# Chunked attention and a normalised feed-forward layer on one core: the z of the last tile turned by VectorE and sixteen transfers instead of by TensorE

## The chip, the cores and the metric

The kernel runs on one core of a Trainium2 chip. The metric is the device time of one execution in microseconds (us). Three runs of the kernel before took 499.17, 499.29 and 499.5 us; the median is 499.29 us. The engines are TensorE (PE in the profile; its weight loads are PEld), VectorE (DVE), ScalarE (ACT), GpSimd (POOL) and SyncE (SP). SP, ACT and POOL each have an instruction queue from which DMA transfers are issued; in the profile these issues are rows of SPq, ACTq and POOLq, or rows of POOL named DMA_DIRECT2D.

## The reference

Attention runs inside chunks of 64 positions, for 8 batches, 8 heads, 576 positions and a head size of 64. Its output, laid out as 4608 tokens of 512 numbers, goes through a feed-forward layer with a SoLU and a layer norm:

```python
scores = scale * q_c @ k_c^T                  # per chunk of 64
attn = softmax(scores);  x = attn @ v_c       # x: 4608 x 512
h = x @ w_in                                  # 4608 x 1024
solu = h * softmax(h)                         # along the row
ln = (solu - mean) / sqrt(var + 1e-06) * g_ln
out = ln @ w_out                              # 4608 x 512
```

All inputs and outputs are float32.

## The kernel before, in words

The 4608 tokens are 36 tiles of 128 tokens, numbered 0 to 35 (`NT` is 36, `P` is 128). Each tile goes through the same stages: scores, softmax and values of its two chunks, then `ffn_in` (the product with `w_in` into the PSUM tile `ph`), `solu_a` and `solu_b` (softmax times h, centred, into the SBUF tile `z`), `variance` (two ScalarE squares and two small GpSimd operations, which give the row factor `r`), the turning of `z` so that its 1024 columns lie on the partitions, `ffn_out` (the product with `w_out` into the PSUM tile `po`), and `store` (ScalarE scales `po` by `r` into `o_sb`, and a transfer writes it out).

Each float32 factor of the two big products is split into a high and a low part, and a product is three passes: high by low, high by high, low by high. So `ffn_out` needs the turned z as two tiles, `ZH` (`z_h` in the profile) and `ZL` (`z_l`). There is one of each for the whole kernel. They are filled in two halves in the last tiles: columns chunks 0 to 3 and 4 to 7 of the eight chunks `fc`. A half of `ZH` can be overwritten only when the products of the tile before have read it.

`ffn_out` of one tile is 24 products of 128x512, three to a chunk `fc`, in the order of `fc`. It is cut into three parts of 8 products each. The list `queue` holds the parts that are not yet issued, and runs three tiles behind `ffn_in`: while tile i is in `ffn_in`, the three parts of tile i-3 are issued between its steps. After the loop over tiles is through, the last `while queue` loop issues what is left, the parts of tiles 33, 34 and 35. In iteration 35 and in this last loop the parts go through `third_ahead`, which after part 1 fills the first half of `ZH` and `ZL` for the next tile (`z_half(m + 1, 0)`), and after part 2 the second half, and then stores the tile. The last tile's `ffn_out` is cut by columns as well: 48 products of 128x256, half of them into a `po` tile and half into a bank of the PSUM tile `TP` (`tp` in the profile), which the function `bank` hands out in turn, two banks in all.

There are two ways from `z` to `ZH` and `ZL`, and `direct(m)` in line 703 says which a tile takes:

- For all tiles but 0, 1 and 35: `z_turn` (line 586). One VectorE transpose turns each 32x32 block in place and writes slot `i % 2` of the SBUF tile `z_b`. Sixteen transfers, eight on SP's queue and eight on POOL's, then carry the blocks to their partitions in the tile `z_t`. `z_b` and `z_t` have two slots each, interleaved in memory, for an even tile and the odd one after it; a pair of tiles is carried at once, after the odd one. Tile 34, whose partner is direct, is carried alone, with half the bytes. `z_split` (line 611) then makes `ZH` with a ScalarE copy and `ZL` with a VectorE subtraction, both reading one slot of `z_t`.
- For tiles 0, 1 and 35: `z_transpose` (line 619). TensorE turns four 128x128 blocks into a bank of `TP`, ScalarE copies the bank into a half of `ZH`, VectorE subtracts for the half of `ZL`; twice, once for each half.

The instructions of each engine stand in the order in which the program writes them: the class `Order` fixes that for TensorE, VectorE, ScalarE, GpSimd and SyncE. Only the transfers that `store_rest` issues through `nc.scalar` have their place chosen by the planner. All these operations are recorded at line 49, the helper, so the rows of the profile are told apart by tile names. Waits between engines are put in by the tile framework from what each instruction reads and writes.

In iteration 35, the order around the change is: `ffn_in(35)`, `solu_a(35)`, part 0 of tile 32, `solu_b(35)`, part 1 of tile 32 with the first half for tile 33, `variance(35)`, part 2 of tile 32 with the second half for tile 33 and the scaling of tile 32, and `store_rest`. Then come tiles 33, 34 and 35 in the last loop.

Of the kernel before, what the change touches and what calls it, by code (L numbers as in the profile page):

```python
# [8 lines left out]
F32 = mybir.dt.float32  # L9
# [48 lines left out]
def chunk_attention_then_solu_ffn(  # L58
# [14 lines left out]
    P = 128  # L73
# [4 lines left out]
    NT = B * S // P  # L78
    NCC = DM // P
    NFC = FF // P  # L80
# [14 lines left out]
    work = ctx.enter_context(tc.tile_pool(name="work", bufs=2))  # L95
# [251 lines left out]
    def load_v(i):  # L347
        V[i] = work.tile([P, H, D], F32, name="v_sb", bufs=4)
        for p0, p1, b, s in tile_parts(i):
            sync.dma_start(  # L350
                V[i][p0:p1], v[b, :, s:s + p1 - p0, :].rearrange("h t d -> t h d")
            )
# [19 lines left out]
    st = {}  # L372
# [43 lines left out]
    def softmax_e(i):  # L416
        e = st[i, "e"]
        act.activation(e, e, AF.Exp, scale=SCALE)

    def softmax_b(i):  # L420
        e = st[i, "e"]
        ssum = small.tile([P, H], F32, name="s_sum")
        if order.on or i in (6, 7):
            dve.tensor_reduce(out=ssum, in_=ES[i % 2], axis=AX.X, op=ALU.add)
        else:
            dve.tensor_reduce(out=ssum, in_=e, axis=AX.X, op=ALU.add)
            dve.tensor_scalar(
                out=ssum, in0=ssum, scalar1=1e-9, scalar2=None, op0=ALU.add
            )
        rinv = small.tile([P, H], F32, name="s_rinv")  # L430
        dve.reciprocal(out=rinv, in_=ssum)
        dve.tensor_tensor(
            out=e, in0=e, in1=rinv.unsqueeze(2).to_broadcast([P, H, CH]), op=ALU.mult,
        )
# [25 lines left out]
    def attn_turn(i):  # L460
        a = st.pop((i, "e"))
        if i % 2 == 0:
            turned["a"] = work.tile([P, 2, 2, H, 32], F32, name="a_b", bufs=1)
        ab = turned["a"]
        dve.transpose(
            out=ab[:, :, i % 2].rearrange("p y h t -> p h y t"),
            in_=a.rearrange("p h (y k) -> p h y k", k=32),
        )
        if i % 2 == 1:
            for c in range(2):  # L470
                for x in range(2):
                    for y in range(2):
                        to, of = c * CH + x * 32, c * CH + y * 32
                        (pool if x == y else sync).dma_start(
                            AT[to:to + 32, y].rearrange("p s h t -> p (s h t)"),
                            ab[of:of + 32, x].rearrange("p s h t -> p (s h t)"),
                        )
# [27 lines left out]
    def x_high(i):  # L505
        xv = attn(i)[:, :, 1].rearrange("p c a t -> p a c t")
        xh = work.tile([P, NCC, P], F32R, name="x_h")
        xl = work.tile([P, NCC, P], F32R, name="x_l")
        xhv, xlv = (x.rearrange("p a (c t) -> p a c t", t=CH) for x in (xh, xl))
        act.copy(xhv, xv)  # L510
        st[i, "x"] = xh, xl
# [6 lines left out]
    def ffn_in(i):  # L518
        xh, xl = st[i, "x"]
        ph = st[i, "h"] = ps_h.tile([P, 2, HALF], F32, name="ph")  # L520

        sums = [(n, cc, m) for n in range(2) for cc in range(NCC) for m in range(3)]
        if i == 0:
            sums.sort(key=lambda s: s[1])
        else:

            sums.sort(key=lambda s: (s[0], s[2] == 2))
        for at, (n, cc, m) in enumerate(sums):
            if i == 0 and at and at % 6 == 0:
                yield  # L530
            cols = slice(n * HALF, (n + 1) * HALF)
            x, w = ((xh, wi_l), (xh, wi_h), (xl, wi_h))[m]
            pe.matmul(
                ph[:, n, :], x[:, cc, :], w[:, cc, cols],
                start=(cc == 0 and m == 0), stop=(cc == NCC - 1 and m == 2),
            )
# [31 lines left out]
    def variance(i):  # L568
        z, esum = st.pop((i, "z"))

        eps = small.tile([P, 1], F32, name="eps")
        act.activation(eps, esum, AF.Square, scale=1e-3, bias=tiny)
        sq = work.tile([P, FF], mybir.dt.bfloat16, name="sq", bufs=1)
        ssq = small.tile([P, 1], F32, name="ssq")
        act.activation(sq, z, AF.Square, scale=1.0 / (FF * 32), accum_out=ssq)
        u = small.tile([P, 1], F32, name="u")
        pool.tensor_tensor(out=u, in0=ssq, in1=eps, op=ALU.add)
        r = small.tile([P, 1], F32, name="r", bufs=7)
        pool.tensor_tensor(out=r, in0=u, in1=mhalf, op=ALU.pow)
        st[i, "n"] = (z, r)  # L580
# [3 lines left out]
    turned = {}  # L584

    def z_turn(i):
        z, _ = st[i, "n"]
        if i % 2 == 0:
            turned["b"] = work.tile([P, 4, 2, NFC, 32], F32, name="z_b", bufs=1)
        zb = turned["b"]  # L590
        dve.transpose(
            out=zb[:, :, i % 2, :, :].rearrange("p q a t -> p a q t"),
            in_=z.rearrange("p (a q c) -> p a q c", q=4, c=32),
        )
        alone = direct(i + 1)
        if i % 2 == 1 or alone:
            zt = work.tile([P, 4, 2, NFC, 32], F32, name="z_t")
            of = slice(0, 1 if alone else 2)
            for x in range(4):
                for y in range(4):  # L600
                    (pool if (x + y) % 2 else sync).dma_start(
                        zt[x * 32:(x + 1) * 32, y, of].rearrange("p s a t -> p (s a t)"),
                        zb[y * 32:(y + 1) * 32, x, of].rearrange("p s a t -> p (s a t)"),
                    )
            for m in (i,) if alone else (i - 1, i):
                st[m, "zr"] = zt
# [4 lines left out]
    def z_split(i, f):  # L611
        zt = st[i, "zr"][:, :, i % 2, :, :].rearrange("p y a t -> p a y t")
        zhv, zlv = (x.rearrange("p a (y t) -> p a y t", t=32) for x in (ZH, ZL))
        act.copy(zhv[:, f], zt[:, f])
        dve.tensor_tensor(
            out=zlv[:, f], in0=zt[:, f], in1=zhv[:, f].bitcast(F32), op=ALU.subtract
        )
# [76 lines left out]
    def load_some(n):  # L694
        for f, *args in loads[:n]:
            f(*args)
        del loads[:n]

    def load_batch(b):
        loads.extend(qk_loads(b))  # L700


    def direct(m):
        return m < 2 or m == NT - 1

    queue = [(m, p) for m in range(NT) for p in range(3)]

# [7 lines left out]
    def third():  # L715
        m, p = queue.pop(0)
        ffn_out(m, p, 3)
        if p == 2:
            store(m)
# [12 lines left out]
    def whole(parts):  # L732
        for _ in parts:
            pass
# [39 lines left out]
    for i in range(first, NT):  # L774
        order.on = i >= ORD
        odd = i % 2 == 1
        if i == first:
            z_turn(i - 1)
            load_batch(next_batch)
            next_batch += 1  # L780
        if i + 3 < NT:
            load_v(i + 3)
        z_split(queue[0][0], slice(0, NFC))
        if not odd:

            if i + 3 < NT:
                softmax_e(i + 3)
                softmax_b(i + 3)
                attn_turn(i + 3)
            if i + 1 < NT:  # L790
                x_high(i + 1)
        load_some(LOADS[0])
        whole(ffn_in(i))

        if odd:
            for m in (i + 1, i + 2):
                if m + 2 < NT:
                    scores(m + 2)
                if m < NT:
                    values(m)  # L800
        whole(solu_a(i))

        def part():
            if i == NT - 1:
                third_ahead()
            else:
                third()

        part()
        if odd:  # L810
            if i + 3 < NT:
                softmax_a(i + 3)
                softmax_e(i + 3)
            if i + 1 < NT:
                x_high(i + 1)
        elif i + 1 < NT:
            x_low(i + 1)
        whole(solu_b(i))
        if odd:
            if i + 1 < NT:  # L820
                x_low(i + 1)
            if i + 3 < NT:
                softmax_b(i + 3)
                attn_turn(i + 3)
        else:
            for m in (i + 4, i + 5):
                if m < NT:
                    turn(m)
        part()
        variance(i)  # L830
        part()
        load_some(LOADS[1])
        if not direct(i):
            z_turn(i)
        store_rest()
        if odd and i + 4 < NT:
            softmax_a(i + 4)
# [34 lines left out]
```

## Time and profile before

| | |
|---|---|
| Median of the runs | 499.29 us (499.17 to 499.5) |
| Profiled execution: its span, first to last instruction | 496.9 us |
| Median of the runs less that span | 2.39 us |
| TensorE busy | 474.8 us, 96% of the span |
| VectorE busy | 382.4 us, 77% |
| ScalarE busy | 263.1 us, 53% |
| GpSimd busy | 144.6 us, 29% |
| Mean granted TensorE clock | 0.998 |

The record of the profiled execution holds its span, and no device time of its own beside it. Times in rows of the timeline and of the chain are microseconds from the span's start. A row of the timeline gives the start, the duration, the engine, the line, the operation with the tile written and the tiles read, the shapes, and how many instructions are merged; in brackets stands the idle time of the engine before it and what ended that. Matmuls are pipelined: a row of 0.39 us follows another after 0.23 us, so the distance between two starts is what a product costs.

### The profile page before, as it was taken

The page shows a single profiled execution, that of the slowest core. Times are in us where ns is not written, and L with a number is a line of the kernel's source. Part 1 is how long each engine was busy: PE and PEld are TensorE (multiplying, and loading weights), DVE is VectorE, ACT ScalarE, POOL GpSimd, SP SyncE. Part 2 cuts the span into 40 slices and gives each one's busy share as a digit, 9 for nine tenths or more (in the row PEclk, how much of TensorE's full clock was granted, in tenths as well). Part 3 has the DMA queues.
Part 4 walks back from the last instruction along what each step waited for, and adds up shares of the span by engine and source line. Part 5 has one row for each costly group of instructions (what it writes and reads, how often), then busy time and mean ns, then how long its engine had stood idle before and what let it go on. Part 6 is the DMA issues. An engine that isn't in the chain of part 4 may idle for free.

```text
span 496.9 us, 11143 instructions
## 1 busy us (share of the span) xinstructions
PE 474.8 (96%) x4232; PEld 387.5 (78%) x4232; DVE 382.4 (77%) x535; ACT 263.1 (53%) x436; POOL 144.6 (29%) x298
## 2 busy tenths in 40 slices
PE   2899699999999999999999999999999999999995
PEld 1577577888888888888888888888888888888875
DVE  2899897778786988787888788887979797944420
ACT  3687784554644455454554545454545454545441
POOL 0134321515050515051414232332323232413300
PEclk9999999999999999999999999999999999999999
DMA  9999894466868678687718596868662525343211
GB/s 263 285 298 246 143 148 89 108 131 165 152 171 150 167 138 199 126 194 126 181 39 196 107 204 128 211 100 197 135 166 63 151 76 139 85 108 106 65 42 42
DMA packets 195908, 72.57 MB, mean 146 GB/s; under 512 B 180048, under 2 KB 180560, under 8 KB 195472
## 3 DMA queue, kind: packets, MB, share of 16 engines
q1 hardware_dynamic: 189008, 58.49, 54.1%
q0 software_dynamic: 6272, 12.60, 9.7%
q8 instruction: 33, 0.54, 0.5%
q10 hardware_dynamic: 576, 0.79, 0.4%
q14 instruction: 19, 0.16, 0.1%
HBM read 37.23 MB, written 9.44 MB: 94 GB/s over the span
## 4 chain that ended last, share of the span: by engine, by line
PE 89%; DVE 4%; ACT 2%; DMA 2%; issue 1%; SPq 1%; POOL 0%; ACTq 0%; DVEq 0%; POOLq 0%
PE po L49 40%; PE ph L49 38%; PE tp L49 6%; PE sx L49 4%; DMA nat<-in_q_dram 2%; SPq L49 1%; DVE w_r L49 1%; DVE w_p L49 1%; ACT z_h L49 1%; ACT attn_t L49 1%; DVE z_l L49 1%; DVE wi_l L49 0%; DVE h_nmax L49 0%; DVE w_a L49 0%; DVE z L49 0%
## 5 line engine op out<-in xcount | busy, mean ns | idle before, releaser
L49 PE MATMUL po<-wo_l,z_h 128*128 128x512 f32 (+1 forms) x288 | 113.4, 394 | 0.1
L49 PE MATMUL ph<-wi_l,x_h 128*128 128x512 f32 x288 | 112.6, 391 | 0.7 <-DVE z L49 0.6
L49 PE MATMUL ph<-wi_h,x_h 128*128 128x512 f32 x288 | 112.1, 389 | 0.0
L49 PE MATMUL po<-wo_h,z_l 128*128 128x512 f32 (+1 forms) x288 | 111.7, 388 | 0.0
L49 PE MATMUL po<-wo_h,z_h 128*128 128x512 f32 (+1 forms) x288 | 111.6, 388 | 0.0
L49 ACT ACTIVATE z<-ph,h_nmax 128x1024 f32<-128x1024 f32 x36 | 40.2, 1117 | 133.2 <-DVE h_nmax L49 132.7
L49 PE MATMUL ph<-wi_h,x_l 128*128 128x512 f32 x288 | 78.0, 389 | 0.0
L49 POOL TENSOR_TENSOR u<-ssq,eps 128x1 f32<-128x1 f32 x36 | 7.2, 199 | 232.8 <-ACT sq L49 232.7
L49 POOL DMA_DIRECT2D z_t<-z_b x136 | 67.9, 506 | 17.6 <-DVE z_b L49 14.8
L49 DVE TENSOR_REDUCE h_nmax<-ph 128x1 f32<-128x1024 f32 x36 | 44.0, 1223 | 33.8 <-PE ph L49 33.8
L49 PEld LDWEIGHTS ph<-wi_l,x_h 128*128 128x128 f32 x288 | 54.1, 188 | 12.2 <-PE sx L49 0.7
L49 PEld LDWEIGHTS po<-wo_l,z_h 128*128 128x128 f32 x288 | 54.1, 188 | 11.8 <-ACT z_h L49 0.5
L49 PEld LDWEIGHTS po<-wo_h,z_l 128*128 128x128 f32 x288 | 54.1, 188 | 11.6 <-DVE z_l L49 0.4
L49 PEld LDWEIGHTS ph<-wi_h,x_l 128*128 128x128 f32 x288 | 54.1, 188 | 11.3
L49 PEld LDWEIGHTS ph<-wi_h,x_h 128*128 128x128 f32 x288 | 54.1, 188 | 11.1
L49 PEld LDWEIGHTS po<-wo_h,z_h 128*128 128x128 f32 x288 | 54.1, 188 | 10.4
L49 DVE TENSOR_TENSOR z_l<-z_t,z_h 128x1024 fp32r<-128x1024 f32 (+1 forms) x35 | 40.7, 1163 | 20.9 <-ACT z_h L49 20.9
L49 DVE SCALAR_TENSOR_TENSOR z<-ph,z 128x1024 f32<-128x1024 f32 x36 | 43.9, 1221 | 14.1 <-ACT z L49 14.1
L49 ACT ACTIVATE z<-z,z_sum 128x1024 f32<-128x1024 f32 x32 | 36.9, 1154 | 22.1 <-DVE z L49 21.6
L49 DVE STREAM_TRANSPOSE z_b<-z 128x1024 f32<-128x1024 f32 x33 | 40.0, 1211 | 3.3 <-ACT z L49 3.1
L49 ACT ACTIVATE o_sb<-po,r 128x512 f32<-128x512 f32 (+1 forms) x36 | 24.3, 675 | 29.2 <-POOL r L49 20.3
L49 ACT ACTIVATE sq<-z 128x1024 bf16<-128x1024 f32 x36 | 37.6, 1043 | 2.2 <-POOL z L49 2.2
(101 smaller groups left out, 638.9 us busy)
## 6 DMA issues: line engine op xcount, KB each, us to landing
out_dram<-o_sb SPq DMA_DIRECT2D x33, 256.0 KB, 2.5
v_sb<-in_v_dram SPq DMA_DIRECT2D x32, 256.0 KB, 4.3
z_t<-z_b SPq DMA_DIRECT2D x128, 64.0 KB, 2.9
z_t<-z_b POOLq DMA_DIRECT2D x128, 64.0 KB, 2.6
q_st<-in_q_dram SPq DMA_DIRECT2D x96, 72.0 KB, 3.2
k_st<-in_k_dram SPq DMA_DIRECT2D x96, 72.0 KB, 3.2
w_raw<-in_moe_w_out_dram SPq DMA_DIRECT2D x4, 1024.0 KB, 6.6
attn_t<-a_b SPq DMA_DIRECT2D x60, 64.0 KB, 3.7
```

Source lines behind the costliest of these rows:

```text
L49: ins = make(*args, **kwargs)
```

## The change

Tile 35 no longer takes the direct way. It shares the `z_t` tile of tile 34, in the other slot, but is carried by sixteen transfers of its own, as tile 34 is by its sixteen. Its `z_turn` is called in iteration 35 after part 1 of tile 32 and ahead of `variance(35)`, so it reads `z` where `solu_b` left it. Tiles 0 and 1 stay direct.

```diff
     def z_turn(i):
-        z, _ = st[i, "n"]
+        z, _ = st.get((i, "n")) or st[i, "z"]
...
-        alone = direct(i + 1)
+        alone = i >= NT - 2
         if i % 2 == 1 or alone:
-            zt = work.tile([P, 4, 2, NFC, 32], F32, name="z_t")
-            of = slice(0, 1 if alone else 2)
+            if i < NT - 1:
+                turned["t"] = work.tile([P, 4, 2, NFC, 32], F32, name="z_t")
+            zt = turned["t"]
+            of = slice(i % 2, i % 2 + 1) if alone else slice(0, 2)
             for x in range(4):
                 for y in range(4):
                     (pool if (x + y) % 2 else sync).dma_start(
...
     def direct(m):
-        return m < 2 or m == NT - 1
+        return m < 2
...
         part()
+        if i == NT - 1:
+            z_turn(i)
         variance(i)
         part()
         load_some(LOADS[1])
-        if not direct(i):
+        if i < NT - 1:
             z_turn(i)
```

## The prediction

> **What bounds the kernel now.** I read the page first, then the chain of waits, then the timeline of the tail engine by engine. The page says which engine sets the end:
>
> ```profile
> span 496.9 us, 11143 instructions
> PE 89%; DVE 4%; ACT 2%; DMA 2%; issue 1%; SPq 1%; POOL 0%; ACTq 0%; DVEq 0%; POOLq 0%
> ```
>
> TensorE carries 89% of the chain. So an edit counts only by what it takes from or adds to TensorE's row of products, and this one touches only the tail. The chain there, start and duration:
>
> ```profile
> 485.94 0.59 ACT z_h L49
> 486.53 0.03 issue
> 486.56 0.70 DVE z_l L49
> 487.26 0.04 issue
> ```
>
> The reader is to see that the chain leaves TensorE for ScalarE and VectorE and comes back to it 0.04 after 487.26, within tile 35. The timeline of TensorE gives the prices; the two rows "tp<-ident,z x4" are the 8 transposes, between the products:
>
> ```profile
> 479.15 0.39 PE L49 MATMUL po<-wo_h,z_l 128*128 128x512 f32 x1
> 479.38 0.39 PE L49 MATMUL po<-wo_l,z_h 128*128 128x512 f32 x1
> ...
> 481.87 0.39 PE L49 MATMUL po<-wo_h,z_l 128*128 128x512 f32 x1
> ...
> 482.78 0.39 PE L49 MATMUL po<-wo_l,z_h 128*128 128x512 f32 x1
> 483.01 0.60 PE L49 MATMUL tp<-ident,z 128*128 128x128 f32 x4
> 483.36 0.48 PE L49 MATMUL po<-wo_h,z_h 128*128 128x512 f32 x1
> ...
> 485.07 0.39 PE L49 MATMUL po<-wo_h,z_l 128*128 128x512 f32 x1
> 485.30 0.60 PE L49 MATMUL tp<-ident,z 128*128 128x128 f32 x4
> 485.66 0.36 PE L49 MATMUL po<-wo_l,z_h 128*128 128x256 f32 x1
> 487.30 0.38 PE L49 MATMUL tp<-wo_l,z_h 128*128 128x256 f32 x1 [1.28 <-DVE z_l L49]
> 487.52 0.28 PE L49 MATMUL po<-wo_h,z_h 128*128 128x256 f32 x1
> 487.64 0.28 PE L49 MATMUL tp<-wo_h,z_h 128*128 128x256 f32 x1
> ...
> 492.92 0.28 PE L49 MATMUL tp<-wo_h,z_l 128*128 128x256 f32 x1
> ```
>
> Tile 34 is the 24 products from 479.38 to 485.07, tile 35 the 48 half products from 485.66 to 492.92. Two paces follow: 16 products start from 479.38 to 482.78, so (482.78 - 479.38) / 15 = 0.227 us each; the fourth to the last half product start from 487.64 to 492.92, 44 steps, 0.120 us each.
>
> **What the change removes.** (1) Two groups of four transposes: the step from 482.78 to 483.36 is 0.58 and that from 485.07 to 485.66 is 0.59, where 0.227 would do: 0.35 + 0.36 = 0.71 us. (2) The wait ahead of the first half product into `tp`: 487.30 - 485.66 - 0.12 = 1.52 us. It ends with the second `z_l` of tile 35, which reads `tp`; without transposes nothing of tile 35 reads `tp`, and the half product has nobody there to wait for. (3) Slower steps just behind the transposes and the wait: the seven steps from 483.36 to 485.07 take 1.71 where 7 x 0.227 = 1.59, and 487.30 to 487.52 is 0.22 where 0.12 would do: 0.12 + 0.10 = 0.22 us. Together **2.45 us**. The same by the dense row: tile 34's last product starts at 479.38 + 23 x 0.227 = 484.60, tile 35's first at 484.82 and its last at 484.82 + 47 x 0.120 = 490.46, against 492.92. What follows the last product (two scalings, two stores) keeps its length.
>
> **What it adds, and whether that is hidden.** One VectorE transpose, sixteen transfers, and ScalarE and VectorE reading `z_t` where they read `tp`. The nearest rows are tile 34's own turn and the splits of tiles 33 and 34:
>
> ```profile
> 462.12 1.25 DVE L49 STREAM_TRANSPOSE z_b<-z 128x1024 f32<-128x1024 f32 x1 [1.22 <-ACT z L49]
> 463.39 4.94 SPq L49 DMA_DIRECT2D z_t<-z_b  x8
> 464.49 3.98 POOL L49 DMA_DIRECT2D z_t<-z_b  x8 [0.27 <-issue]
> 471.81 1.15 ACT L49 ACTIVATE z<-z,z_sum 128x1024 f32<-128x1024 f32 x1 [1.30 <-DVE z L49]
> 472.87 0.60 ACT L49 CAST z_h<-z_t 128x512 fp32r<-128x512 f32 x1
> 473.51 0.69 DVE L49 TENSOR_TENSOR z_l<-z_t,z_h 128x512 fp32r<-128x512 f32 x1 [1.73 <-ACT z_h L49]
> 473.53 0.50 PE L49 MATMUL po<-wo_l,z_h 128*128 128x512 f32 x1
> 474.59 0.39 PE L49 MATMUL po<-wo_l,z_h 128*128 128x512 f32 x1
> 475.26 0.69 DVE L49 TENSOR_TENSOR z_l<-z_t,z_h 128x512 fp32r<-128x512 f32 x1 [1.06 <-ACT z_h L49]
> 479.35 0.62 ACT L49 CAST z_h<-z_t 128x512 fp32r<-128x512 f32 x1 [2.10 <-PE po L49]
> 480.00 0.69 DVE L49 TENSOR_TENSOR z_l<-z_t,z_h 128x512 fp32r<-128x512 f32 x1 [2.03 <-ACT z_h L49]
> ```
>
> z of tile 35 is complete at 471.81 + 1.15 = 472.96. On VectorE the transpose stands behind the `z_l` of tile 33's first half, which ends at 473.51 + 0.69 = 474.20, so it runs from 474.20 to 475.45. Behind it is `z_l` of tile 33's second half, due at 475.26: 0.19 us late, so it ends at 476.14. Its first reader is tile 33's fifteenth product; the first starts at 473.53, the fourth at 474.59, the fifteenth 11 x 0.227 later, at 477.09. Free.
>
> The transfers: tile 34's first SP issue came 0.02 after its transpose ended. Here SP issues from 475.47, eight in 4.94 us, the last at 475.47 + 7 x 0.62 = 479.8. POOL takes 3.98 for eight. From issue to landing, from the list of DMA issues in the tail and, below it, the summary of all `z_t` instructions of the kernel:
>
> ```profile
> z_t<-z_b SPq DMA_DIRECT2D x8, 32.0 KB, 1.9
> z_t<-z_b POOLq DMA_DIRECT2D x8, 32.0 KB, 1.7
> DMA to landing us min/median/max: 1.7/2.8/4.5
> ```
>
> The likely landing is 479.8 + 1.9 = 481.7; I take it since those rows have the same size and neighbours. The far end is 479.8 + 4.5 = 484.3.
>
> The first `z_h` of tile 35 overwrites a half that tile 34's twelfth product, at 481.87, reads last. At the tile boundary before, `z_h` at 479.35 came 0.20 after the start of the product at 479.15, so TensorE frees the half at 482.07, after the likely landing. From `z_h` to the end of `z_l` are 480.00 - 479.35 + 0.69 = 1.34 us, so both are there at 483.41. TensorE asks for that `z_h` at 484.82 and for that `z_l` four half products later, at 485.30; the landing may slip to 485.30 - 1.34 = **483.96** before TensorE waits at all. By the far landing, 484.3, it waits 0.34 us and the gain is 2.1. The second half: freed at 484.60 + 0.20 = 484.80, `z_h` ready at 485.42, `z_l` at 486.14, asked for at 484.82 + 24 x 0.120 = 487.70. Free.
>
> Two queues are passed, and each instruction on them is late by the issues ahead of it:
>
> ```profile
> 475.06 0.56 POOL L49 TENSOR_TENSOR r<-u,mhalf 128x1 f32<-128x1 f32 x1
> ```
>
> On POOL, `u` and `r` of tile 35 now stand behind eight issues: `r` ends a little after 475.47 + 3.98 + 0.56 = 480.0 instead of at 475.62, and its first user is a scaling behind the last products, after 490. On SP the store of tile 32 moves behind the eight issues too, to 475.47 + 4.94 = 480.4. The two `o_sb` buffers take turns, so the scaling of tile 34, due when its last product is through at 484.80, needs that store landed; it has 4.4 us for that, and no product of tile 34 or 35 waits for that scaling. On ScalarE the `z_h` that waits for the landing has only the second `z_h` and tile 34's scaling behind it, both due no sooner than 484.80. All of it costs nothing while the landing is before 483.96.
>
> The sum: 496.9 - 2.45 = 494.45 us for the span. The median of the runs is 2.39 us above the span shown, which I carry over unchanged: 499.29 - 2.45 = **496.84 us**.
>
> **Rivals.** *A, the slots are not kept apart (slower).* Tile 34's split reads slot 0 of `z_t`, and in program order it now stands behind the transfers into slot 1 of the same tile. The slots are interleaved; if the waits are made for the whole stretch that the read covers, tile 34's first `z_h` must wait for tile 35's transfers.
>
> ```profile
> 476.63 0.62 ACT L49 CAST z_h<-z_t 128x512 fp32r<-128x512 f32 x1 [0.82 <-PE po L49]
> 484.26 0.69 DVE L49 TENSOR_TENSOR z_l<-tp,z_h 128x512 fp32r<-128x512 f32 x1 [3.57 <-ACT z_h L49]
> ```
>
> It would start at 481.7 instead of 476.63. At tile 33 `z_h` led the first product by 473.53 - 472.87 = 0.66 us, so tile 34 would start at 482.36 instead of 479.38, 2.98 late, and its third product waits for `z_l` as tile 33's did: there the first three products took 474.59 - 473.53 = 1.06 us where 0.68 would do. That is 2.98 + 0.38 = 3.36 lost for 2.45 won: 500.2 us, and 502.8 with the far landing. It becomes a loss once the transfers land after 480.8. For it: the half product at 487.30 waited until the second `z_l` was done, though by the code its bank is that of the first, done at 484.26 + 0.69 = 484.95; so waits are wider than the data there. Against it: `z_h` at 476.63 overwrote its half of `ZH` while tile 33 was still reading the other half (until 479.15), so SBUF parts are told apart, if not interleaved ones.
>
> *B, the transfers land late.* If they land 1 us after 483.96 the time is 497.8; all is lost only with a landing at 486.4, 6.6 us after the last issue, against 4.5 for the slowest of the kernel. Against it: tile 34's sixteen transfers, of the same size and issued in the same way, landed in 1.9 and 1.7. The Trainium skill, page "VectorE: DVE Perf Modes", section "Rules for kernel authors", says to turn a 128x128 block on TensorE where a result in PSUM will do, which it does here, and so speaks against this change. The rows bear it out for latency only: from the transposes to `z_h` it took 485.94 - 485.30 = 0.64 us, while the other way takes 481.7 - 474.20 = 7.5; but it has from 472.96 to 483.96.
>
> *C, the wait stays.* If the first half product into `tp` still waited for tile 35's second `z_l` (486.14), 486.18 - 484.94 = 1.24 would be lost again: 498.1 us. Against it: tile 34's first product at 479.38 did not wait for the `z_l` that began at 480.00.
>
> *D, no change.* The end is set by something that the chain does not show, 499.3 us. The chain's unbroken run on TensorE speaks against it.
>
> **How the numbers follow.** Forecast 0.74, A 0.11, B 0.07, C 0.05, D 0.03. Runs of this kernel differ by 0.33 us, and 0.2% (1.0 us) is about what a measurement can tell from no change. The forecast, nearly all of B (0.06) and half of C (0.03) are faster by more: 0.83. C's and B's rest, D and A with the earliest landing (0.04) are within it: 0.10. A with later landings is slower: 0.07. The range goes from 496.4 (the runs' scatter and the paces' rounding below the sum) to 498.2, which takes in the far landing, most of B and C; A and D are left out.
>
> **What would show it.** Right: no `tp<-ident,z` rows in the tail, a VectorE transpose near 474.2, last `z_t` landing before 484, TensorE starting tile 35 near 484.8 with no gap until 490.5. Wrong: tile 34's first `z_h` past 480 with a releaser DMA (A), a gap on TensorE ahead of tile 35 ended by `z_h` (B), or ahead of the first half product into `tp` (C).

## The result, and the profile after

Five runs of the changed kernel have a median of 496.39 us (495.26 to 496.82), five of the kernel before 499.17 us (498.42 to 499.5). The ratio is 0.995, with a 95% interval of 0.9938 to 0.9963: 1.8 to 3.1 us less. The median lies at the lower end of the stated range, 496.4 to 498.2.

The span of the profiled execution fell from 496.9 to 493.5 us, by more than the prediction's 2.45. The tail shows what the change did. The chain of waits after, start and duration:

```profile
471.94 0.61 ACT z_h L49
472.55 0.04 issue
472.59 11.56 PE po L49 x49
484.15 0.12 PE tp L49
484.27 0.12 PE po L49
...
487.87 0.97 PE po L49 x8
```

Before, the chain left TensorE at 485.91 and came back at 487.30. Now it stays on TensorE from tile 33's first product to the scalings behind the last products. TensorE's timeline at tiles 34 and 35:

```profile
478.44 0.39 PE L49 MATMUL po<-wo_l,z_h 128*128 128x512 f32 x1
...
483.65 0.39 PE L49 MATMUL po<-wo_h,z_l 128*128 128x512 f32 x1
483.88 0.28 PE L49 MATMUL po<-wo_l,z_h 128*128 128x256 f32 x1
483.99 0.28 PE L49 MATMUL tp<-wo_l,z_h 128*128 128x256 f32 x1
...
489.51 0.28 PE L49 MATMUL tp<-wo_h,z_l 128*128 128x256 f32 x1
```

Tile 34 takes (483.65 - 478.44) / 23 = 0.227 us a product, tile 35 (489.51 - 483.88) / 47 = 0.120 a half product: both are dense, with nothing between them. From tile 33's first to tile 35's last product it was 492.92 - 473.53 = 19.39 us, and is 489.51 - 472.59 = **16.92**: 2.47 us less. What was added, in the same window, lies beside that:

```profile
473.18 1.24 DVE L49 STREAM_TRANSPOSE z_b<-z 128x1024 f32<-128x1024 f32 x1
474.34 0.67 DVE L49 TENSOR_TENSOR z_l<-z_t,z_h 128x512 fp32r<-128x512 f32 x1
474.44 4.95 SPq L49 DMA_DIRECT2D z_t<-z_b  x8
474.71 3.91 POOL L49 DMA_DIRECT2D z_t<-z_b  x8 [7.20 <-DVE z_b L49]
475.69 0.62 ACT L49 CAST z_h<-z_t 128x512 fp32r<-128x512 f32 x1 [0.82 <-PE po L49]
476.34 0.69 DVE L49 TENSOR_TENSOR z_l<-z_t,z_h 128x512 fp32r<-128x512 f32 x1 [1.33 <-DMA z_t<-z_b]
478.91 0.56 POOL L49 TENSOR_TENSOR r<-u,mhalf 128x1 f32<-128x1 f32 x1
481.13 0.62 ACT L49 CAST z_h<-z_t 128x512 fp32r<-128x512 f32 x1 [1.51 <-PE po L49]
```

The rows at 475.69 and 481.13 are the first `z_h` of tiles 34 and 35. The first began while tile 35's transfers were still being issued; the second waited for TensorE, not for a transfer. The row at 476.34, the first `z_l` of tile 34, names a transfer as what ended its wait. But it began 0.03 us after its `z_h` ended (475.69 + 0.62 = 476.31), as in the kernel before (477.28 against 476.63 + 0.62 = 477.25), and most of tile 35's transfers had not been issued by then: they did not hold it up.

The other 0.94 us of the span lie ahead of tile 33 (473.53 against 472.59), and 0.93 of them ahead of tile 0's first product, where the two programs are alike. The first product into `ph`, before and then after:

```profile
30.14 0.39 PE L49 MATMUL ph<-wi_l,x_h 128*128 128x512 f32 x1
```

```profile
29.21 0.39 PE L49 MATMUL ph<-wi_l,x_h 128*128 128x512 f32 x1
```

Tile 33's first product came between 472.54 and 474.05 in the seven other profiles below whose program is the same up to there; the latest, 474.05, belongs to the run with the other bank, whose clock was lowered for a time early on (last section). Nothing that the change touches lies there, so this part is taken as scatter between executions, and the readings below go by the stretch from tile 33's first to tile 35's last product.

### The profile page after: what moved, and what is told of

It reads as the page before. It is cut to its first block, busy times and chain, and to the rows that moved or that the text cites. A ratio compares the mean times of both kernels' runs of the same rounds, so it can differ in the third digit from the quotient of the medians.

```text
span 493.5 us, 11163 instructions
## 1 busy us (share of the span) xinstructions
PE 473.3 (96%) x4224; PEld 386.3 (78%) x4224; DVE 383.1 (78%) x536; ACT 263.1 (53%) x436; POOL 148.6 (30%) x306
## 4 chain that ended last, share of the span: by engine, by line
PE 89%; DVE 4%; ACT 2%; DMA 2%; issue 1%; SPq 1%; POOL 0%; ACTq 0%; DVEq 0%; POOLq 0%
PE po L49 40%; PE ph L49 39%; PE tp L49 6%; PE sx L49 4%; DMA nat<-in_q_dram 2%; SPq L49 1%; DVE w_r L49 1%; DVE w_p L49 1%; ACT attn_t L49 1%; DVE wi_l L49 0%; ACT z_h L49 0%; DVE h_nmax L49 0%; DVE z_l L49 0%; DVE w_a L49 0%; DVE z L49 0%
## 5 line engine op out<-in xcount | busy, mean ns | idle before, releaser
L49 POOL DMA_DIRECT2D z_t<-z_b x144 | 71.6, 505 | 24.8 <-DVE z_b L49 23.1
L49 DVE TENSOR_TENSOR z_l<-z_t,z_h 128x1024 fp32r<-128x1024 f32 (+1 forms) x37 | 42.1, 1137 | 24.1 <-ACT z_h L49 22.7
L49 DVE STREAM_TRANSPOSE z_b<-z 128x1024 f32<-128x1024 f32 x34 | 41.2, 1211 | 3.3 <-ACT z L49 3.1
L49 ACT CAST z_h<-z_t 128x1024 fp32r<-128x1024 f32 (+1 forms) x37 | 35.8, 969 | 6.5 <-PE po L49 6.5
```

The lines of the kernel that those rows point to most:

```text
L49: ins = make(*args, **kwargs)
```

## The experiments

**The wait alone taken away, transposes kept.** The kernel before with:

```diff
-                ps_o.tile([P, DM], F32, name="po") if x == 0 else bank()
+                ps_o.tile([P, DM], F32, name="po") if x == 0
+                else ps_h.tile([P, 2, HALF], F32, name="ph")[:, 0]
```

> The kernel before, with the transposes kept; only the second column half of tile 35's last product goes into the PSUM tile ph, which is free by then, instead of into a bank of tp. It leaves nothing out. My theory (the gain is the transposes' 0.71 us plus 0.12 us of slower steps, and the wait of the first half product into tp with the slow step behind it, 1.62 us): the wait is gone and nothing else, so from tile 33's first product to tile 35's last it is 19.39 - 1.62 = 17.8 us, and the time is 1.6 us below before. Rival (the product waits for z_l itself, not for tp): the gap of 1.5 us stays, 19.4 us, same time as before.

Measured: 17.83 us for the stretch; ratio to before 0.9978 (0.9965 to 0.9991). TensorE's timeline around the second group of transposes:

```profile
485.13 0.60 PE L49 MATMUL tp<-ident,z 128*128 128x128 f32 x4
485.49 0.36 PE L49 MATMUL po<-wo_l,z_h 128*128 128x256 f32 x1
485.69 0.28 PE L49 MATMUL ph<-wo_l,z_h 128*128 128x256 f32 x1
```

The half product at 485.69, whose counterpart before started 1.64 us after its neighbour, now follows after 0.20. The wait was for `tp` and not for `z_l`; without it 19.39 - 17.83 = 1.56 us are gained. The step of 0.20 where 0.12 would do stays: it belongs to the transposes.

**The other bank.** The kernel before with:

```diff
-                ps_o.tile([P, DM], F32, name="po") if x == 0 else bank()
+                ps_o.tile([P, DM], F32, name="po") if x == 0 else (bank(), bank())[1]
```

> The kernel before, with one bank skipped, so that the second half of tile 35's last product lies in the other bank of tp. If the wait is for whatever reads the tile tp, whichever bank, the gap ahead of that product stays at 1.5 us and ends with the second z_l. If the wait is by bank and my count of the banks was off by one, the product now waits for the first z_l only, done long before, and the gap is gone: 17.8 us from tile 33's first to tile 35's last product instead of 19.39.

Measured, in one run: 19.40 us for the stretch, and the same gap in TensorE's timeline:

```profile
486.18 0.36 PE L49 MATMUL po<-wo_l,z_h 128*128 128x256 f32 x1
487.82 0.39 PE L49 MATMUL tp<-wo_l,z_h 128*128 128x256 f32 x1 [1.28 <-DVE z_l L49]
```

With the banks exchanged the wait is the same 1.64 us and ends with the same second `z_l`. Whichever bank the product writes, it waits for the last reader of the tile `tp`. The time of this run, 499.23 us, is not compared: its clock was lowered early in the execution, as the last section shows.

**The transposes alone put back.** The changed kernel with:

```diff
+        if p > 0 and m + 1 == NT - 1:
+            pt = bank().rearrange("p (a t) -> p a t", t=P)
+            for a in range(4):
+                fc = 4 * (p - 1) + a
+                pe.transpose(pt[:, a, :], st[m + 1, "n"][0][:, fc * P:(fc + 1) * P], ident)
         if p == 1 and m + 1 < NT:
```

> The changed kernel, with the eight transposes of tile 35 put back on TensorE at the places that they had before (behind parts 1 and 2 of tile 34), their result read by nobody. Theory: TensorE pays for them as it did before, 0.71 us for the two groups and 0.12 us for the slower steps behind the first, so 16.92 + 0.83 = 17.75 us from tile 33's first to tile 35's last product, and no gap ahead of the first half product into tp, since no VectorE instruction reads tp there. Rival (the transposes slip into gaps of TensorE): 16.9 us.

Measured: 17.82 us; ratio to before 0.9961 (0.995 to 0.9972). The transposes cost 17.82 - 16.92 = 0.90 us; what the expectation missed of it, 0.07, is the step behind the second group, 485.31 - 485.11 = 0.20 where 0.12 would do:

```profile
484.75 0.60 PE L49 MATMUL tp<-ident,z 128*128 128x128 f32 x4
485.11 0.36 PE L49 MATMUL po<-wo_l,z_h 128*128 128x256 f32 x1
485.31 0.28 PE L49 MATMUL tp<-wo_l,z_h 128*128 128x256 f32 x1
```

The two parts, each done alone, make 1.56 + 0.90 = 2.46 us, the 2.47 of the change. And they differ from each other in what they leave: nobody reads `tp` here, and the half product into it does not wait.

**The turn at its usual place.** The changed kernel with:

```diff
-        if i == NT - 1:
-            z_turn(i)
         variance(i)
...
-        if i < NT - 1:
-            z_turn(i)
+        z_turn(i)
```

> The changed kernel, with tile 35's turn at the place that the other tiles have, behind variance and behind the second half for tile 33. Theory (slack): the VectorE transpose starts near 475.0 instead of 473.2, the last transfer lands near 482.5, the first z_h of tile 35 then starts there instead of at 481.1, its z_l ends near 483.9 and is asked for at 484.35: no wait on TensorE, 16.9 us from tile 33's first to tile 35's last product, same time as the changed kernel. Rival (the early place is what the gain rests on): a gap ahead of tile 35, over 0.5 us.

Measured: 16.93 us; ratio to before 0.9956 (0.9941 to 0.9971). ScalarE's first `z_h` of tile 35, and TensorE's first products of it:

```profile
483.25 0.62 ACT L49 CAST z_h<-z_t 128x512 fp32r<-128x512 f32 x1 [3.25 <-DMA z_t<-z_b]
```

```profile
484.26 0.28 PE L49 MATMUL po<-wo_l,z_h 128*128 128x256 f32 x1
...
484.73 0.30 PE L49 MATMUL po<-wo_h,z_l 128*128 128x256 f32 x1
484.87 0.28 PE L49 MATMUL tp<-wo_h,z_l 128*128 128x256 f32 x1
```

Now `z_h` does wait for the transfers (the releaser is a DMA), and TensorE still has no gap: only the step behind 484.73, the first reader of `z_l`, is 0.14 instead of 0.12. This is the edge of the slack. It came 483.25 - 472.97 = 10.28 us after tile 33's first product (at 472.97); the prediction put the edge at 483.96 - 473.53 = 10.43.

**All sixteen transfers on SP.** The changed kernel with:

```diff
-                    (pool if (x + y) % 2 else sync).dma_start(
+                    (pool if (x + y) % 2 and i < NT - 1 else sync).dma_start(
```

> The changed kernel, with all sixteen transfers of tile 35 on SP's queue. Theory (slack with an edge): sixteen issues take 9.9 us from 474.44, the last is issued at 483.7 and lands at 485.6; z_h of tile 35 starts there, 2.6 us past the 483.0 from which TensorE waits, so a gap of about 2.6 us ahead of tile 35, ended by z_h and z_l, and 19.5 us from tile 33's first to tile 35's last product: the gain is gone, 499 us. Rival (the landing does not matter much, some other engine sets tile 35's start): 17 to 18 us, at most 1 us slower than the changed kernel.

Measured: 21.32 us, ratio to before 1.006 (1.0038 to 1.0083): slower than before, and worse than either theory said. TensorE's timeline, and its busy time and granted clock (the PEclk column, the third from the right) in three stretches:

```profile
483.76 0.39 PE L49 MATMUL po<-wo_h,z_l 128*128 128x512 f32 x1
486.92 0.58 PE L49 MATMUL po<-wo_l,z_h 128*128 128x256 f32 x1 [2.77 <-ACT z_h L49]
487.30 0.42 PE L49 MATMUL tp<-wo_l,z_h 128*128 128x256 f32 x1
...
490.08 0.28 PE L49 MATMUL po<-wo_h,z_h 128*128 128x256 f32 x1
```

```profile
483.90:486.90 3.00, 0.25 (x2) 0.00 (x0) 0.00 (x0) 0.65 (x2) 0.00 (x0) 0.96 0.53 188
486.90:489.40 2.50, 2.48 (x11) 2.48 (x12) 1.29 (x2) 1.07 (x2) 0.00 (x0) 0.50 0.28 109
490.10:494.10 4.00, 4.00 (x35) 4.00 (x34) 0.00 (x0) 0.47 (x1) 0.00 (x0) 1.00 0.00 0
```

The gap is 486.92 - 483.76 - 0.23 = 2.93 us, near the 2.6 expected. The rest is new: behind the gap the granted clock is 0.50, and half products come every 0.21 us instead of 0.12 until about 490. Tile 35 took 494.02 - 486.92 = 7.10 us from its first to its last product instead of 5.63: 1.47 us. Of these, 1.22 lie in the thirteen steps from 487.30 to 490.08 (2.78 us, where 13 x 0.12 = 1.56 would do), and the rest in the first step, 0.38. Gap and slow steps make 4.40, the whole of 21.32 - 16.92.

**Fourteen on SP, two on POOL**, to part the gap from the clock. The same line with `(i < NT - 1 or x == 0)` in the place of `i < NT - 1`.

> The changed kernel with fourteen of tile 35's transfers on SP's queue and two on POOL's. With sixteen on SP, TensorE stood still for 2.8 us ahead of tile 35, its granted clock then read 0.50 for 2.5 us, and 21.3 us passed from tile 33's first to tile 35's last product instead of the 19.5 that the gap alone explains. Two issues fewer are 1.25 us earlier, so the gap is near 1.5 us. If the clock falls only behind a long stand, as the 1.28 us ahead of tile 35 in the kernel before suggest, it stays at 1.00 and the stretch is 16.9 + 1.6 = 18.5 us. If any such gap halves it, 20 us.

Measured, in one run (497.28 us): 18.89 us for the stretch. TensorE's timeline at the gap, and the stretch behind it with its clock:

```profile
484.08 0.39 PE L49 MATMUL po<-wo_h,z_l 128*128 128x512 f32 x1
485.94 0.39 PE L49 MATMUL po<-wo_l,z_h 128*128 128x256 f32 x1 [1.47 <-ACT z_h L49]
486.17 0.28 PE L49 MATMUL tp<-wo_l,z_h 128*128 128x256 f32 x1
```

```profile
486.00:490.00 4.00, 4.00 (x31) 3.81 (x32) 1.22 (x2) 1.00 (x2) 0.00 (x0) 1.00 0.21 79
```

The gap is 485.94 - 484.08 - 0.23 = 1.63 us and the clock behind it 1.00. The stretch is 1.97 longer than the changed kernel's; the 0.34 beside the gap are slower steps among the first five half products, of 0.23, 0.26 and 0.22 us, where `z_l` comes in late: VectorE began it at 485.92, and its first reader started at 486.67. So the transfers cost somewhat more than they are late past the edge while the clock stays at 1.00, and more again where it falls.

**Tile 33's first half made earlier**, a version meant to beat the changed kernel too. The changed kernel, in iteration 35, with part 1 of tile 32 and the first half for tile 33 between the two steps of `solu_b(35)`:

```diff
-        whole(solu_b(i))
+        rest = solu_b(i)
+        next(rest)
+        if i == NT - 1:
+            part()
+        whole(rest)
...
-        part()
         if i == NT - 1:
             z_turn(i)
+        else:
+            part()
```

> The changed kernel, with part 1 of tile 32 and the first half for tile 33 written ahead of the ScalarE half of solu_b(35), so that ScalarE makes the first z_h of tile 33 while it waits for VectorE's z, and not behind its 1.15 us activation of z. If TensorE's wait at tile 33's first products (from the last product of tile 32, 0.46 us to the first and 1.06 us from the first to the fourth, where 0.23 and 0.68 would do) comes only from that order, it is gone: 0.6 us from tile 32's last product to tile 33's fourth are saved, 16.5 us from tile 33's first to tile 35's last product, and the time is 0.6 us below the changed kernel. Rival: the z of tile 35 comes later on ScalarE or VectorE and eats what is won, or z_l of tile 33 is held by VectorE's z operation: less than 0.3 us.

Measured: 16.51 us, and from tile 32's first to tile 35's last product 21.95 instead of 22.59; ratio to before 0.9935 (0.9917 to 0.9953). It was run again beside the changed kernel:

> The changed kernel once more, for a comparison on one chip with the version that fills tile 33's halves earlier: 16.9 us from tile 33's first to tile 35's last product, about 2.5 us below before.

> The changed kernel with the first half for tile 33 written ahead of the ScalarE half of solu_b(35), as in the run before it: 16.5 us from tile 33's first to tile 35's last product, and 0.6 us below the changed kernel beside it, if the 0.64 us that the trace showed ahead of and inside tile 33 are a gain in time; rival: no difference from the changed kernel beyond 0.2 us.

Measured, changed kernel: 16.93 us, median 495.6 us, ratio to before 0.994 (0.9923 to 0.9956). This version: 16.51 us, median 495.0 us, ratio 0.9927 (0.9912 to 0.9942). TensorE at the passage from tile 32 to tile 33, in the changed kernel and then in the first run of this version:

```profile
472.13 0.39 PE L49 MATMUL po<-wo_h,z_l 128*128 128x512 f32 x1
472.59 0.50 PE L49 MATMUL po<-wo_l,z_h 128*128 128x512 f32 x1
472.93 0.40 PE L49 MATMUL po<-wo_h,z_h 128*128 128x512 f32 x1
473.32 0.50 PE L49 MATMUL po<-wo_h,z_l 128*128 128x512 f32 x1
```

```profile
474.27 0.39 PE L49 MATMUL po<-wo_h,z_l 128*128 128x512 f32 x1
474.50 0.39 PE L49 MATMUL po<-wo_l,z_h 128*128 128x512 f32 x1
474.72 0.39 PE L49 MATMUL po<-wo_h,z_h 128*128 128x512 f32 x1
474.95 0.39 PE L49 MATMUL po<-wo_h,z_l 128*128 128x512 f32 x1
```

The steps of 0.46, 0.34 and 0.39 us are all 0.23 now. The trace shows the 0.64 us gained in both runs, and the medians side by side differ by 0.6; the intervals of the two ratios overlap, so of the times alone only the gain over the kernel before is clear.

## Why the prediction was right

**The sum held.** 2.45 us were forecast and the stretch shows 2.47. Moved by the 0.94 us by which this execution was ahead, tile 35's first and last product start at 484.82 and 490.45; the forecast was 484.82 and 490.46. The terms were sized from the right rows, with one shift between them: of the step from 485.66 to 487.30, 0.08 us was put down to the wait (it is part of the 1.52 of term 2), and the run without the wait showed that it comes with the transposes. So they cost 0.90 where the prediction's rows give 0.71 + 0.12 = 0.83, and the wait 1.56 where they give 1.52 + 0.10 = 1.62.

**The cover was there.** The last transfer's landing was forecast 8.2 us after tile 33's first product; in the trace the last of the eight SP issues starts at about 474.44 + 7 x 0.62 = 478.8, and those transfers landed 1.9 us after their issue (the median), which makes 8.1 us. The slack to the edge, over 2 us, was real: a turn 1.75 us later (475.31 - 472.97 = 2.34 us behind tile 33's first product, against 473.18 - 472.59 = 0.59) cost nothing, and transfers past the edge opened a gap. So the early place of the turn, which the prediction priced at nothing lost, is also nothing won. On POOL `r` went to 478.91, on SP the store of tile 32 behind the eight issues, and no one waited for either, as forecast.

**Rival A fell.** Tile 34's first `z_h` started at 475.69, while the transfers into the other slot were being issued until 479.39. The interleaved slots of `z_t` are kept apart. The evidence that had spoken for A was read rightly, but it holds for `tp` and not for `z_t`: in `tp` waits are for the whole tile, as the run with the other bank showed.

**Rival B** did not come about, but its mechanism is real: its edge was some 0.15 us off, and its price, one us for each us of lateness, is too low: a gap of 1.63 us cost 1.97 at a clock of 1.00, and one of 2.93 cost 4.40 with the clock at 0.50, which the prediction left out. The rule of the Trainium skill, page "VectorE: DVE Perf Modes", section "Rules for kernel authors", to turn 128x128 blocks on TensorE where PSUM will do, did not hold for the time here: TensorE, which bounds the tail, paid 0.90 us for the turning and 1.56 for its PSUM tile, and the longer way (473.18 to 481.13) was covered.

**Rival C** fell: the step into `tp` is 483.99 - 483.88 = 0.11 us. **D** (an end set by something outside the chain) fell too: the time fell, by about what the chain gave.

**What was off.** The median came out at 496.39, 0.45 us below the forecast, and the difference of the medians, 2.78, above its 2.45; the interval of 1.8 to 3.1 holds both. The step of the sum that did not hold is the carrying over of "the median of the runs is 2.39 us above the span". In the five runs of the changed kernel the time was 1.76 to 1.82 us above the span of the same execution. By that the execution profiled before, with 496.9, stood near 498.7 us, and the 2.39 held some 0.6 us of scatter between runs. That scatter was also taken too small: the three runs of before lay within 0.33 us, while 13 runs beside the first experiments spread from 497.35 to 499.84, with a median of 498.19. So the forecast of the difference rests on the mechanism, but that the time itself came out as near as 0.45 us is partly luck: the changed kernel, run again, had a median of 495.6, which is 1.2 us below the forecast and 0.8 below the range.

## What to carry to other kernels

Ask of every small operation on the engine that bounds a stage not only how long it runs but which buffer it leaves occupied: here the wait for the PSUM tile behind the transposes cost more than the transposes. A path that takes some twelve times as long (7.5 us against 0.64 in the prediction's rows) is the better one where it has the time; work out the latest moment at which its result may come, and how far the likely one is from it. And compare two profiles from an event behind the loads: the scatter ahead of it, 1.5 us here, is over half of what was to be measured.

## What the runs showed of the hardware

Two things were not expected. Behind a stand of TensorE (a stretch in which it has no product) of 2.77 us the granted clock was 0.50 from about 486.7 to 490.0, and half products took 0.21 us instead of 0.12; behind 1.47 us, and behind the 1.28 us of the kernel before, it stayed at 1.00. In the four runs with the longer stand the mean clock of the execution was 0.995 to 0.997; in all the others for which it is on record it was 0.998 to 1.000, but for one. That one, the run with the other bank, has 0.992, and its trace shows that the length of a stand does not decide alone. Its TensorE near tile 1, far ahead of the tail, and the stretch with its clock:

```profile
50.33 0.66 PE L49 MATMUL tp<-ident,nat 128*128 128x128 f32 x4 [1.56 <-ACT z_h L49]
52.39 1.55 PE L49 MATMUL tp<-ident,nat 128*128 128x128 f32 x8 [0.78 <-DVE z_l L49]
```

```profile
53.00:59.50 6.50, 5.53 (x22) 4.22 (x21) 5.26 (x8) 3.83 (x6) 1.68 (x2) 0.50 0.85 143
```

Between the two stands TensorE had four transposes and 32 products of 64x64. The ten other traces have the same two stands at this place, and a clock of 1.00 behind them. Behind the last product of the kernel, too, the clock falls at no fixed time: about 2.0 us after that product's end in the kernel before (493.20 to 495.24), 4.7 in the run with the turn at its usual place (490.18 to 494.91). So a stand of 1.47 us is not shown to be safe, and what decides is open. The Trainium skill, page "TensorE: Matmul & The Clock Gate", section "Why this matters for your kernels", warns of idle gaps above about 3 us; here 2.8 us was enough, and in one execution of eleven the clock fell behind stands of 1.56 and 0.78 us.

And a wait for a PSUM tile of two banks covered both banks, while waits for interleaved slots of a tile in SBUF went slot by slot. A half product into a tile of its own, `ph`, did not wait. Whether the wait for the second bank is only in how the program's waits are made, or would be needed for another reason, was not tried.
